# One 64-row-tiled phase per chunk for scores, q/k transposes and x transposes in a gated-attention plus squared-relu kernel

## The chip, the cores and the metric

The kernel runs on one core of one Trainium2 chip. The time is device time of one execution in microseconds (us); lower is better. Every kernel was run four times, three of them interleaved with runs of the kernel before on the same chip. A ratio is the mean time of one kernel's fast runs over the mean of the other's of the same rounds, so it is not quite the ratio of the medians that stand beside it. The rounds ran on different chips, and the median of the kernel before was 196.66 to 198.9 us in them, so runs of different rounds are compared by their ratios or by their profiled spans. Times inside a run are read from its one profiled execution, in which the span from first to last instruction is about 2 us shorter than the device time.

Engines are named as the profile names them: PE (matmul), PEld (weight load), DVE (vector), ACT (activation), POOL, SP. PSUM is the memory that PE writes, in banks of 2 KiB per partition.

## The reference, cut to what matters

```python
# B=4, H=8, S=768, D=48: a gated linear attention, 32 recurrences over 768 tokens
for t in range(S):
    state = alpha[:, :, t, :, None] * state + einsum('bhd,bhe->bhde', k[:, :, t], v[:, :, t])
    y[:, :, t] = einsum('bhd,bhde->bhe', q[:, :, t], state)
x = y.transpose(0, 2, 1, 3).reshape(3072, 384)
h = x @ w_in                  # 384 -> 2048
out = maximum(h, 0)**2 @ w_out  # 2048 -> 384
```

Of the kernel before, what the change touches and what calls it, by code (L numbers as in the profile page):

```python
# [8 lines left out]
FP32 = mybir.dt.float32  # L9
BF16 = mybir.dt.bfloat16  # L10
AF = mybir.ActivationFunctionType
ALU = mybir.AluOpType
PSUM = bass.MemoryType.PSUM
# [6 lines left out]
class Slots:  # L20


    def __init__(self, bufs):
        self.bufs, self.release = bufs, []
# [7 lines left out]


class Op:
    def __init__(self, eng, dur, emit, deps=(), prio=0.0, takes=None, gives=None, lat=0.2, at=0.0):
        self.eng, self.dur, self.emit = eng, dur, emit
        self.deps, self.prio = [d for d in deps if d is not None], prio
        self.takes, self.gives, self.lat, self.at = takes, gives, lat, at
        self.start = self.done = None


class Plan:
# [13 lines left out]
    def ready(self, op):  # L56
        t = op.at
        for d in op.deps:
            if d.done is None:
                return None  # L60
            t = max(t, d.done)
        if op.takes is not None:
            best = None
            for sl in op.takes:
                f = sl.free_at()
                if f is not None and (best is None or f < best):
                    best, op.slot = f, sl
            if best is None:
                return None
            t = max(t, best)  # L70
        return t

    def run(self, gate):
        free = self.free
        while any(self.pending.values()):
            best = None
            for eng, ops in self.pending.items():
                t0 = free.get(eng, 0.0)
                pick = None
                fifo = eng in ("DMA",)  # L80
                for op in (ops[:1] if fifo else ops):
                    if not gate(op):
                        continue
                    r = self.ready(op)
                    if r is None:
                        continue
                    key = (max(r, t0), op.prio)
                    if pick is None or key < pick[0]:
                        pick = (key, op)
                if pick is not None and (best is None or pick[0][0] < best[0]):  # L90
                    best = (pick[0][0], eng, pick[1])
            assert best is not None, "nothing can run"
            t, eng, op = best
            for e in op.durs:
                self.pending[e].remove(op)
            op.eng, op.dur = eng, op.durs[eng]
            op.start = t + getattr(op, "late", 0.0)
            free[eng] = t + op.dur
            if eng == "OUT":
                free["DMA"] = max(free.get("DMA", 0.0), t) + op.dur  # L100
            op.done = t + op.dur + op.lat
            if op.takes is not None:
                self.ready(op)
                op.slot.release.append(op.gives if op.gives is not None else op)
            self.order.append(op)
            self.on_pick(op)
        self.order.sort(key=lambda o: o.start)
# [3 lines left out]
def kernel(  # L111
# [10 lines left out]
    nc = tc.nc  # L122
    B, H, S, D = q.shape
    HD = H * D
    P = 128
    DP = 64
    NP = H // 2
# [3 lines left out]
    KT = d_model // P  # L131
    FT = d_ff // P
    NT = n_tok // P
# [14 lines left out]

    ps_sc = ctx.enter_context(tc.tile_pool(name="ps_sc", bufs=1, space=PSUM))
    ps_st = ctx.enter_context(tc.tile_pool(name="ps_st", bufs=1, space=PSUM))  # L150
    banks = [ctx.enter_context(tc.tile_pool(name=f"bank{i}", bufs=1, space=PSUM)) for i in range(5)]

    nc.scalar.preload_act_table_set("natural_log_exp_and_others")

# [2 lines left out]
    ident_bf = consts.tile([P, P], BF16)  # L157
# [12 lines left out]
    w_in_b = consts.tile([P, KT, d_ff], BF16)  # L170
    w_out_b = consts.tile([P, FT, d_model], BF16)

    NBUF = 4
    L_s = big.tile([P, NBUF, H, DP], BF16)
    nc.gpsimd.memset(L_s[:, :, :, D:], 0.0)
    qA_s = big.tile([P, NBUF, H, DP], BF16)
    nc.gpsimd.memset(qA_s[:, :, :, D:], 0.0)
    kI_s = big.tile([P, NBUF, H, DP], BF16)
    nc.gpsimd.memset(kI_s[:, :, :, D:], 0.0)
    ae_s = big.tile([P, NBUF, NP, 2], FP32)  # L180
    nc.vector.memset(ae_s, 0.0)  # L181
    xT_big = big.tile([P, KT, n_tok], BF16)

    def pin(ins):
        tc.keep_in_program_order(ins)
# [4 lines left out]
    def tr(*a):  # L190
        pin(nc.tensor.transpose(*a))  # L191

    plan = Plan()
    sl_sc = Slots(1)
# [3 lines left out]
    GLA_BANKS = sl_bank[0:2]  # L198
    M1_BANKS = sl_bank[2:5]
    M2_BANKS = sl_bank[4:1:-1]  # L200

    def psum(op, shape, dt):
        i = op.slot.bank
        return banks[i].tile(shape, dt, name=f"bank{i}")
    X_SLACK = 0.3
    LD = 1.02
# [3 lines left out]
    def add(eng, dur, emit, *deps, **kw):  # L210
        return plan.add(Op(eng, dur, emit, deps, **kw))
# [26 lines left out]
    def hold_w(d):  # L238
        def e_hold():
            pin(nc.gpsimd.tensor_copy(hold, d["qt"][:, 0, 0:1]))  # L240
        w_gate[:] = [add("POOL", 0.1, e_hold, d["ld_qt"], prio=-6.0)]

    def hold_x(d, i):
# [4 lines left out]
            pin(nc.gpsimd.tensor_copy(d["at"][:, 0, 0:1], w_out_b[:, j, 0:1]))  # L248
        d["go"] = add("POOL", 0.1, e_hold, w_out_ready[i][0], prio=-6.0)

    C = [dict() for _ in range(NT)]
    state = {}

    def add_loads(s):
        d = C[s]
        b, c = divmod(s, NCH)
        for nm, src in srcs:
            def ld(nm=nm, src=src):
                if nm not in d:
                    d[nm] = loads.tile([P, H, D], FP32, name=nm)  # L260
                pin(nc.sync.dma_start(out=d[nm], in_=src[b, c]))
            prev = C[s - LB]["use_" + nm] if s >= LB else None
            d["ld_" + nm] = add("DMA", LD, ld, prev, d.get("go") if nm == "at" else None, lat=2.0, at=0.6)

    def add_chunk(s):
        d = C[s]
        b, c = divmod(s, NCH)
        i = s % NBUF
        L, qA, kI, ae = L_s[:, i], qA_s[:, i], kI_s[:, i], ae_s[:, i]
        old = C[s - NBUF].get("end") if s >= NBUF else None  # L270
        g = dict(prio=-10.0 + s * 0.01)
        last = c == NCH - 1
# [48 lines left out]
        mq = d["use_qt"] = add("DVE", 0.47, e_qA, a_, d["ld_qt"], old, **g)  # L321
        mk = d["use_kt"] = add("DVE", 0.47, e_kI, ai, d["ld_kt"], old, **g)

        def e_p1():
# [2 lines left out]
                tr(d["pT"][:, p, :], qA[:, 2 * p:2 * p + 2, :], ident_bf)  # L327
            for p in range(NP):
                tr(d["pT"][:, NP + p, :], kI[:, 2 * p:2 * p + 2, :], ident_bf)
        p1 = plan.add(Op("PE", 0.47, e_p1, [mq, mk], takes=GLA_BANKS, **g))  # L330

        def e_cp():
            d["qkT"] = work.tile([P, 2 * NP, P], BF16, name="qkT")
            pin(nc.vector.tensor_copy(d["qkT"], d["pT"]))  # L334
        cp = add("DVE", 0.61, e_cp, p1, **g)
        p1.gives = cp

        def e_p2():
            sc = d["sc"] = ps_sc.tile([P, 2, NP, P], FP32, name="sc")
            t = d["qkT"]  # L340
            for p in range(NP):
                for hh in range(2):
                    sl = slice(64 * hh, 64 * hh + 64)
                    mm(sc[:, hh, p, :], lhsT=t[sl, NP + p, :], rhs=t[sl, p, :], start=True, stop=True)
        p2 = plan.add(Op("PE", 0.42, e_p2, [cp], takes=[sl_sc], **g))

        def e_sm(hh):
            if hh == 0:
                d["sm"] = work.tile([P, 2, NP, P], BF16, name="sm")
            pin(nc.vector.tensor_mul(d["sm"][:, hh], d["sc"][:, hh], utri_b.to_broadcast([P, NP, P])))  # L350
        sm0 = add("DVE", 0.6, lambda: e_sm(0), p2, **g)
        sm1 = add("DVE", 0.6, lambda: e_sm(1), p2, sm0, **g)
        p2.gives = sm1

        ps = None
        if not last:
            def e_ps():
# [3 lines left out]
                for p in range(NP):  # L361
                    mm(st[:, p, :], lhsT=kI[:, 2 * p:2 * p + 2, :], rhs=d["vb"][:, 2 * p:2 * p + 2, :],
                       start=(c == 0 and p == 0), stop=True, skip_group_check=True)
            prev = C[s - 1].get("sb") if s else None
            if c == 0 and s:
                prev = C[s - 2]["sb"]
            ps = plan.add(Op("PE", 0.17, e_ps, [mk, vb, ae1, prev], **g))
# [27 lines left out]
        xn = add("ACT", 0.37, e_xn, p3, **g)  # L395
        p3.gives = xn

        def e_p4():
            d["px"] = psum(p4, [P, KT, P], BF16)
            for j in range(KT):  # L400
                tr(d["px"][:, j, :], d["xn"][:, j * P:(j + 1) * P], ident_bf)
        p4 = plan.add(Op("PE", 0.18, e_p4, [xn], takes=GLA_BANKS, **g))

        def e_xT():
            pin(nc.vector.tensor_copy(xT_big[:, :, s * P:(s + 1) * P], d["px"]))  # L405
        d["x"] = add("DVE", 0.27, e_xT, p4, prio=-9.0, lat=0.2 + X_SLACK)
        p4.gives = d["x"]
        d["end"] = d["x"]


    GN = [4, 1, 1, 2, 2, 2, 2, 2, 2, 2, 2, 2]
# [80 lines left out]
    for d in DMA_ORDER + [s for s in range(NT) if s not in DMA_ORDER]:  # L492
        if d == "i":
            load_w_in(len(w_in_ready))
        elif d == "o":
            load_w_out(len(w_out_ready))
        else:
            if d in HOLD_X:
                hold_x(C[d], HOLD_X[d])
            add_loads(d)  # L500
            add_chunk(d)
            if d in HOLD_W:
                hold_w(C[d])
    b1 = b2 = None
    FIRST_PARTS = [[0, 1], [2, 3]]
    for g in range(NG):
# [10 lines left out]
                b2 = add_moe2(g, tt, b2, {}, range(NQ), M2_LAST if g >= NG - 2 else M2_BANKS if g < M1_ALT else [sl_bank[4]])  # L517
        sq[(g, "free")] = b2

    LEAD = 4  # L520

    def gate(op):
        s = getattr(op, "gla", None)
        if s is not None:
            return s <= LEAD + (prog["m1"] + prog["m2"]) / 5.12
        return True
# [54 lines left out]
```

## The kernel before: the parts that the change touches

The tokens are worked in 24 chunks of 128. A chunk of attention goes through these steps, each of which takes PSUM space from one of two banks (`GLA_BANKS`, banks 0 and 1), except for scores and state, which have their own:

- P0: cumulative sums of log alpha (PE), then `A`, `Ainv` and two small `ae` by exp (ACT); then `qA = q*A`, `kI = k*Ainv` (DVE).
- q/k transposes: eight 128x128 transposes (PE) into one bank, then a copy `qkT` (DVE).
- scores: eight matmuls with 64 rows each (PE), then masking `sm` (DVE).
- product: state times q, and `sm` times v (PE), then the copy `xn` (ACT).
- x transposes: three 128x128 transposes of `xn` (PE), then the copy `xT_big` (DVE).

Beside them run the two large matmuls: the first one, `w_in` with `xT_big` (256 columns in most groups), with relu on ACT (`r`) and the square on DVE (`gT`); the second one, `w_out` with `gT` (384 columns). A small planner in the kernel simulates the engines with planned durations and fixes the order of instructions on each engine ahead of time. The hardware then runs each engine's list in that order and waits on semaphores.

```python
banks = [ctx.enter_context(tc.tile_pool(name=f"bank{i}", bufs=1, space=PSUM)) for i in range(5)]
GLA_BANKS = sl_bank[0:2]
def psum(op, shape, dt):
    i = op.slot.bank
    return banks[i].tile(shape, dt, name=f"bank{i}")      # one tile per bank and use
...
def e_p1():                                               # q/k transposes
    d["pT"] = psum(p1, [P, 2 * NP, P], BF16)
    for p in range(NP):
        tr(d["pT"][:, p, :], qA[:, 2 * p:2 * p + 2, :], ident_bf)
    for p in range(NP):
        tr(d["pT"][:, NP + p, :], kI[:, 2 * p:2 * p + 2, :], ident_bf)
...
def e_p2():                                               # scores: pairs of 64 rows
    for p in range(NP):
        for hh in range(2):
            sl = slice(64 * hh, 64 * hh + 64)
            mm(sc[:, hh, p, :], lhsT=t[sl, NP + p, :], rhs=t[sl, p, :], start=True, stop=True)
...
LEAD = 4                                                  # chunks that P0 may run ahead
```

## Time and profile before

| what | value | view |
|---|---|---|
| device time, median | 198.9 us (197.17 to 199.66, 4 runs) | result |
| PE busy | 94% of the span of 195.0 us | page, part 1 |
| chain that ended last | 87% PE | page, part 4 |
| one chunk in the steady part | 7.07 us; PE 7.07, DVE 5.92, ACT 5.68 | windows |
| eight q/k transposes / three x transposes | 0.45 / 0.17 us | chain, start to next |

These are lines of the page of the kernel before: the span, the busy time of each engine, the busy share of PE in 40 slices in tenths, the granted PE clock in tenths, and the chain of work that ended last, by engine (followed back from the last instruction, at each step to what it had waited for).

```profile
span 195.0 us, 5164 instructions
PE 184.1 (94%) x1920; PEld 130.4 (67%) x1924; DVE 138.2 (71%) x360; ACT 130.9 (67%) x379; POOL 24.0 (12%) x49
PE   7888799999999996999999999999999999999993
PEclk9999999999999999999999999999999999999999
PE 87%; DVE 6%; ACT 3%; issue 1%; ACTq 0%
```

The windows view of the kernel before gives the busy time of each engine in a stretch (with the number of instructions), the clock, and the DMA share:

```profile
core 0: us, PE busy (x) PEld busy (x) DVE busy (x) ACT busy (x) POOL busy (x), PEclk, DMA share, GB/s
103.38:110.45 7.07, 7.07 (x83) 5.40 (x81) 5.92 (x16) 5.68 (x16) 0.64 (x1) 1.00 0.97 202
```

From about 78 us on PE never rests, so PE work taken away should be time taken away. DVE has some 1.2 us and ACT 1.4 us to spare per chunk.

Two stretches of the PE timeline of the kernel before follow (start, duration, engine, line, operation, number of instructions, and in brackets the idle time and what ended it). The first is the steady part, from one P0 to the product; the second is chunk 2 to 3 near the start:

```profile
113.95 0.33 PE L188 MATMUL bank<-L_s,utri_b 128*128 128x384 bf16 x1
114.11 0.24 PE L188 MATMUL bank<-ones_col,L_s 128*128 128x1 bf16 x4
114.22 0.49 PE L188 MATMUL bank<-xT_big,w_in_b 128*128 128x256 bf16 x3
114.54 0.33 PE L188 MATMUL bank<-sb,qkT 128*128 128x96 bf16 x4
...
18.77 0.33 PE L188 MATMUL bank<-sb,qkT 128*128 128x96 bf16 x4
18.94 0.56 PE L188 MATMUL bank<-vb,sm 128*128 128x48 bf16 x8
19.70 0.40 PE L191 MATMUL bank<-ident_bf,qA_s 128*128 128x128 bf16 x4 [0.20 <-DVE qA_s L317]
```

In the steady part the product follows P0 after 0.59 us without a wait, although ACT reads P0's bank until 114.88 us. The product is in the other bank. Near the start, the wait of the q transposes ends with their own input (`qA_s`); what they also wait for in the program is an exp that reads their own bank, and it came earlier.

### The profile page before, as it was taken

What the parts mean: (1) busy time and instruction counts of PE and PEld (TensorE: products, weight loads), DVE (VectorE), ACT (ScalarE), POOL (GpSimd) and SP (SyncE); (2) the same over time, 40 slices, a digit from 0 to 9 for tenths busy, and PEclk for the clock granted to TensorE, in tenths of its full rate; (3) what the DMA queues carried; (4) which work ended last, traced back from release to release, by engine and by line L of the source; (5) the groups of instructions that cost most, each with busy time, mean ns of one, the idle gap of its engine ahead of it and who ended that gap; (6) DMA issues with size and microseconds to landing.
All of it is one profiled execution on the core that took longest, in us unless ns stands there. A gap on an engine that the chain in (4) does not pass through costs nothing.

```text
span 195.0 us, 5164 instructions
## 1 busy us (share of the span) xinstructions
PE 184.1 (94%) x1920; PEld 130.4 (67%) x1924; DVE 138.2 (71%) x360; ACT 130.9 (67%) x379; POOL 24.0 (12%) x49
## 2 busy tenths in 40 slices
PE   7888799999999996999999999999999999999993
PEld 2455444666776775777877777777777787777661
DVE  0588646735999699769998888788888788744300
ACT  3366269527797599488877977877887777565510
POOL 5127300401111111120110110110010000000000
PEclk9999999999999999999999999999999999999999
DMA  6998999899999989998999999601101101110022
GB/s 122 218 216 138 174 197 181 131 196 251 219 216 181 196 180 209 184 216 188 214 224 202 201 204 224 134 33 45 40 5 40 40 3 40 44 40 26 20 79 81
DMA packets 107033, 27.07 MB, mean 139 GB/s; under 512 B 100352, under 2 KB 107008, under 8 KB 107008
## 3 DMA queue, kind: packets, MB, share of 16 engines
q1 hardware_dynamic: 103296, 23.60, 56.2%
q0 software_dynamic: 3712, 3.15, 10.9%
q8 instruction: 15, 0.25, 0.5%
q14 instruction: 10, 0.08, 0.2%
HBM read 25.17 MB, written 4.72 MB: 153 GB/s over the span
## 4 chain that ended last, share of the span: by engine, by line
PE 87%; DVE 6%; ACT 3%; issue 1%; ACTq 0%
PE bank L188 75%; PE bank L191 8%; PE sc L188 3%; DVE sm L350 2%; PE st L188 1%; DVE qA_s L317 1%; DVE st L371 1%; DVE kI_s L320 1%; DVE xT_big L405 1%; ACT r L443 1%; DVE qkT L334 1%; ACT A L298 0%; ACT xn L394 0%; ACT sb L376 0%; ACT L_s L275 0%
## 5 line engine op out<-in xcount | busy, mean ns | idle before, releaser
L443 ACT ACTIVATE r<-bank 128x256 bf16<-128x256 f32 (+2 forms) x192 | 69.1, 386 | 21.9 <-PE bank L188 19.1
L188 PE MATMUL bank<-xT_big,w_in_b 128*128 128x256 bf16 (+2 forms) x575 | 79.5, 272 | 0.9 <-ACT r L443 0.4
L188 PE MATMUL bank<-w_out_b,gT 128*128 128x384 bf16 x384 | 74.7, 326 | 0.0
L449 DVE TENSOR_TENSOR gT<-r 128x256 bf16<-128x256 bf16 (+2 forms) x192 | 55.3, 306 | 20.3 <-ACT r L443 19.1
L188 PEld LDWEIGHTS <-w_in_b 128*128 128x128 bf16 x576 | 48.7, 97 | 15.6 <-issue 1.5
L188 PEld LDWEIGHTS <-gT 128*128 128x128 bf16 x384 | 36.2, 98 | 16.9
L350 DVE TENSOR_TENSOR sm<-sc,utri_b 128x512 bf16<-128x512 f32 x48 | 32.4, 685 | 4.5 <-PE sc L188 4.4
L281 POOL CAST vb<-vt 128x384 bf16<-128x384 f32 x24 | 13.9, 577 | 101.9 <-PE bank L188 58.7
L334 DVE COPY qkT<-bank 128x1024 bf16<-128x1024 bf16 x24 | 16.6, 690 | 7.2 <-PE bank L191 7.1
L317 DVE TENSOR_TENSOR qA_s<-qt,A 128x384 bf16<-128x384 f32 x24 | 13.6, 567 | 8.7 <-ACT A L298 8.7
L480 ACT COPY ob<-bank 128x384 f32<-128x384 f32 x22 | 10.5, 478 | 11.0 <-PE bank L188 10.1
L188 PEld LDWEIGHTS <-qkT 64*128 64x128 bf16 (+1 forms) x272 | 10.9, 95 | 9.8 <-DVE gT L449 3.4
L298 ACT ACTIVATE A<-bank 128x384 bf16<-128x384 f32 x24 | 11.8, 493 | 7.7 <-PE bank L188 7.7
L376 ACT CAST sb<-st 128x384 bf16<-128x384 f32 x20 | 9.6, 478 | 10.8 <-DVE st L371 10.7
L394 ACT CAST xn<-bank 128x384 bf16<-128x384 f32 x24 | 11.5, 480 | 5.0 <-PE bank L188 4.9
L275 ACT ACTIVATE L_s<-at 128x384 bf16<-128x384 f32 x24 | 12.5, 524 | 3.6 <-DMA at<-in_alpha_dram 3.5
L320 DVE TENSOR_TENSOR kI_s<-kt,Ainv 128x384 bf16<-128x384 f32 x24 | 13.5, 564 | 0.2
L188 PE MATMUL bank<-warm 128*128 128x512 bf16 x33 | 11.2, 478 | 1.3 <-DVE ae_s L181 1.3
L302 ACT ACTIVATE Ainv<-bank 128x384 bf16<-128x384 f32 x24 | 11.9, 496 | 0.0
L188 PE MATMUL sc<-qkT 64*128 64x128 bf16 x192 | 9.5, 219 | 2.0 <-DVE qkT L334 2.0
L405 DVE COPY xT_big<-bank 128x384 bf16<-128x384 bf16 x24 | 8.4, 351 | 4.0 <-PE bank L191 3.9
L371 DVE TENSOR_TENSOR st<-st,ae_s 128x384 f32<-128x384 f32 x20 | 11.1, 556 | 0.0
(39 smaller groups left out, 128.2 us busy)
## 6 DMA issues: line engine op xcount, KB each, us to landing
at<-in_alpha_dram SPq DMA_DIRECT2D x24, 192.0 KB, 3.8
qt<-in_q_dram SPq DMA_DIRECT2D x24, 192.0 KB, 3.7
kt<-in_k_dram SPq DMA_DIRECT2D x24, 192.0 KB, 3.8
vt<-in_v_dram SPq DMA_DIRECT2D x24, 192.0 KB, 3.9
out_dram<-ob SPq DMA_DIRECT2D x24, 192.0 KB, 2.3
w_in_b<-in_moe_w_in_dram POOLq DMA_DIRECT2D x4, 384.0 KB, 7.3
w_out_b<-in_moe_w_out_dram POOLq DMA_DIRECT2D x4, 384.0 KB, 8.1
```

The source lines that it names most:

```text
L188: pin(nc.tensor.matmul(*a, **kw))
L191: pin(nc.tensor.transpose(*a))
L275: pin(nc.scalar.activation(L[:, :, 0:D], d["at"], AF.Ln))
L281: pin(nc.gpsimd.tensor_copy(d["vb"], d["vt"]))
L302: pin(nc.scalar.activation(d["Ai"], d["pm"][:, 0:HD].rearrange("p (h d) -> p h d", h=H), AF.Exp, scale=-1.0))
L317: pin(nc.vector.tensor_mul(qA[:, :, 0:D], d["qt"], d["A"]))
L320: pin(nc.vector.tensor_mul(kI[:, :, 0:D], d["kt"], d["Ai"]))
L334: pin(nc.vector.tensor_copy(d["qkT"], d["pT"]))
L350: pin(nc.vector.tensor_mul(d["sm"][:, hh], d["sc"][:, hh], utri_b.to_broadcast([P, NP, P])))
L371: pin(nc.vector.tensor_mul(st4, st4, bcast(ae, D)))
L443: pin(nc.scalar.activation(box["r"][:, 0:n], box["ph"][:, 0:n], AF.Relu))
L449: pin(nc.vector.tensor_mul(gT[g][:, f, 0:n], box["r"][:, 0:n], box["r"][:, 0:n]))
```

## The change

The intent: from chunk 11 on, the full-size transposes become pairs of half-token (64-row) transposes that PE runs at once, as it already does for the scores. Because a switch between 128-row and 64-row instructions costs time (PE is 96 ns late at the entry in these traces), they are put into one phase with the scores. Each half writes its own bank, so one phase needs banks 0 and 1 together; the change therefore makes both banks one tile `G`, so that one DVE copy can read both. A tile is a buffer that the kernel declares by name; waits between the instructions that use a tile are put in when the program is built. P0 may run a chunk further ahead (`LEAD` 5, six chunk buffers).

```diff
-    banks = [ctx.enter_context(tc.tile_pool(name=f"bank{i}", bufs=1, space=PSUM)) for i in range(5)]
+    ps_g = ctx.enter_context(tc.tile_pool(name="ps_g", bufs=1, space=PSUM))
+    banks = [None, None] + [ctx.enter_context(tc.tile_pool(name=f"bank{i}", bufs=1, space=PSUM)) for i in range(2, 5)]
-    NBUF = 4
+    NBUF = 6
+    G = ps_g.tile([P, 2, 512], FP32, name="G")
+    G_b = G.bitcast(BF16)
+    G_T = G_b[:, :, 0:8 * 64].rearrange("p h (t c) -> p h t c", c=64)
+    G_x = G_b[:, :, 8 * 64:11 * 64].rearrange("p h (t c) -> p h t c", c=64)
     def psum(op, shape, dt):
         i = op.slot.bank
+        if i < 2:
+            if dt == FP32:
+                return G[:, i, :]
+            return G_b[:, i, 0:shape[1] * P].rearrange("p (t c) -> p t c", c=P)
+    M0 = 11
... (the separate transposes and scores are kept for earlier chunks) ...
+        def e_ph():
+            if nx:
+                for t in range(2 * NP):
+                    src = (nx["qA"] if t < NP else nx["kI"])[:, 2 * (t % NP):2 * (t % NP) + 2, :]
+                    for h in range(2):
+                        sl = slice(64 * h, 64 * h + 64)
+                        tr(G_T[:, h, t, :], src[sl], ident_bf[sl, sl])
+            for t in range(KT):
+                for h in range(2):
+                    sl = slice(64 * h, 64 * h + 64)
+                    tr(G_x[:, h, t, :], pv["xn"][sl, t * P:(t + 1) * P], ident_bf[sl, sl])
+            d["e_sc"]()
... (the planner learns of operations that take both banks; x copy priority -9 to -11) ...
-    LEAD = 4
+    LEAD = 5
```

`G` is used in all 24 chunks, not only from chunk 11 on.

More of the change, by code (lines that the diff above doesn't have):

```diff
@@ L34, with __init__ @@
 class Op:
-    def __init__(self, eng, dur, emit, deps=(), prio=0.0, takes=None, gives=None, lat=0.2, at=0.0):
+    def __init__(self, eng, dur, emit, deps=(), prio=0.0, takes=None, gives=None, lat=0.2, at=0.0, all_of=None):
         self.eng, self.dur, self.emit = eng, dur, emit
@@ L38, in __init__ @@
         self.takes, self.gives, self.lat, self.at = takes, gives, lat, at
+        self.all_of = all_of
         self.start = self.done = None
@@ L61, in ready @@
             t = max(t, d.done)
+        if op.all_of is not None:
+            for sl, _ in op.all_of:
+                f = sl.free_at()
+                if f is None:
+                    return None
+                t = max(t, f)
         if op.takes is not None:
@@ L104, in run @@
                 op.slot.release.append(op.gives if op.gives is not None else op)
+            for sl, gives in op.all_of or ():
+                sl.release.append(gives)
             self.order.append(op)
@@ L329, in e_p1 @@
                 tr(d["pT"][:, NP + p, :], kI[:, 2 * p:2 * p + 2, :], ident_bf)
-        p1 = plan.add(Op("PE", 0.47, e_p1, [mq, mk], takes=GLA_BANKS, **g))
+        d["mq"], d["mk"], d["qA"], d["kI"] = mq, mk, qA, kI
+        joint_t, joint_s = s > M0, s >= M0
+        if not joint_t:
+            p1 = plan.add(Op("PE", 0.47, e_p1, [mq, mk], takes=GLA_BANKS, **g))
         def e_cp():
             d["qkT"] = work.tile([P, 2 * NP, P], BF16, name="qkT")
-            pin(nc.vector.tensor_copy(d["qkT"], d["pT"]))
-        cp = add("DVE", 0.61, e_cp, p1, **g)
-        p1.gives = cp
+            if joint_t:
+                pin(nc.vector.tensor_copy(d["qkT"].rearrange("p t (h c) -> p h t c", h=2), G_T))
+            else:
+                pin(nc.vector.tensor_copy(d["qkT"], d["pT"]))
+        if joint_t:
+            cp = d["cp"] = add("DVE", 0.63, e_cp, C[s - 1]["ph"], C[s - 2]["x"] if "x" in C[s - 2] else None, **g)
+        else:
+            cp = d["cp"] = add("DVE", 0.61, e_cp, p1, **g)
+            p1.gives = cp
         def e_p2():
@@ L344, in e_p2 @@
                     mm(sc[:, hh, p, :], lhsT=t[sl, NP + p, :], rhs=t[sl, p, :], start=True, stop=True)
-        p2 = plan.add(Op("PE", 0.42, e_p2, [cp], takes=[sl_sc], **g))
+        if not joint_s:
+            p2 = plan.add(Op("PE", 0.42, e_p2, [cp], takes=[sl_sc], **g))
+        else:
+            p2 = d["ph"] = Op("PE", 0.20, None, **g)
+        d["e_sc"] = e_p2
         def e_sm(hh):
@@ L352, in add_chunk @@
         sm1 = add("DVE", 0.6, lambda: e_sm(1), p2, sm0, **g)
+        d["sm1"] = sm1
         p2.gives = sm1
@@ L401, in e_p4, with add_phase @@
                 tr(d["px"][:, j, :], d["xn"][:, j * P:(j + 1) * P], ident_bf)
-        p4 = plan.add(Op("PE", 0.18, e_p4, [xn], takes=GLA_BANKS, **g))
-        def e_xT():
-            pin(nc.vector.tensor_copy(xT_big[:, :, s * P:(s + 1) * P], d["px"]))
-        d["x"] = add("DVE", 0.27, e_xT, p4, prio=-9.0, lat=0.2 + X_SLACK)
+        d["xn_op"] = xn
+        joint_x = M0 - 1 <= s < NT - 1
+        if joint_x:
+            p4 = d["ph_x"] = Op("PE", 0.0, None)
+        else:
+            p4 = plan.add(Op("PE", 0.18, e_p4, [xn], takes=GLA_BANKS, **g))
+        def e_xT():
+            xT = xT_big[:, :, s * P:(s + 1) * P]
+            if joint_x:
+                pin(nc.vector.tensor_copy(xT.rearrange("p t (h c) -> p h t c", h=2), G_x))
+            else:
+                pin(nc.vector.tensor_copy(xT, d["px"]))
+        d["x"] = add("DVE", 0.27, e_xT, p4, prio=-11.0, lat=0.2 + X_SLACK)
         p4.gives = d["x"]
         d["end"] = d["x"]
+    def add_phase(s):
+        d, nx, pv = C[s], C[s + 1] if s + 1 < NT else None, C[s - 1]
+        op = d["ph"]
+        def e_ph():
[10 more added lines that the diff above has]
+            d["e_sc"]()
+        op.emit = e_ph
+        op.deps = [d["cp"], pv["xn_op"]] + ([nx["mq"], nx["mk"]] if nx else [])
+        op.dur = 0.41 + 0.09 + (0.23 if nx else 0.0)
+        last = nx["cp"] if nx else pv["x"]
+        op.all_of = [(GLA_BANKS[0], last), (GLA_BANKS[1], last), (sl_sc, d["sm1"])]
+        plan.add(op)
+        pv["x"].deps = [op]
+        if nx:
+            nx["cp"].deps = [op, pv["x"]]
     GN = [4, 1, 1, 2, 2, 2, 2, 2, 2, 2, 2, 2]
@@ L503 @@
                 hold_w(C[d])
+    for s in range(M0, NT):
+        add_phase(s)
     b1 = b2 = None
```

## The prediction

> **What bounds it now.** The page gives PE 94% of 195.0 us; the chain of waits that ended last is 87% PE. By windows of one chunk (103.38 to 110.45 us, 110.45 to 117.52), PE is busy 7.07 of 7.07 us, DVE 5.92, ACT 5.65, clock 1.00, so from about 78 to 172 us PE is the limit and 7.07 us the period. Before that PE has gaps: in the timeline some 2.1 us between 74.9 and 77.7 us (P0, then state, x and q/k transposes, each waiting for ACT), and 2.9 us between 45 and 65 us.
>
> **What the change saves.** In the chain a chunk's eight q/k transposes take 0.45 us, its three x transposes 0.17: 56 ns each. The scores, already 64-row pairs, start 3 ns apart within a pair and 56 ns from pair to pair (N=128). As the Trainium skill says, "TensorE: Matmul & The Clock Gate", Part 3 (row tiles run concurrently, starts about 4 ns apart). Smallest pitches seen: 25 ns (one column), 26 ns (48 columns). Estimate for a 64-column pair: 29 ns, up to 40 if weight loads of the two halves don't overlap fully. Eleven pairs then cost 0.32 to 0.44 us instead of 0.62: 0.2 to 0.29 us a chunk, over 12 to 13 chunks about 3.2 us. Drains don't change: the skill's "TensorEngine Tiling", Key Properties, says a mode switch drains; here about 96 ns before and 120 ns after the scores, once a chunk, in both kernels. DVE copies should keep 0.69 and 0.35 us. The larger lead moves one P0 ahead of 15 matmuls near 74 us and should remove about 1.3 of the 2.1 us gap.
>
> **What it adds.** Banks 0 and 1 become one tile G. In the built program waits now cross the banks. (a) Steady: in five chunks P0 is followed by three 256-column matmuls (0.33 us), then the state-times-q matmul, which now waits for the exp A in the other bank. A ended 0.93 us after P0's start in this trace, the matmul came at 0.59: a stall of 0.38 to 0.5 us; one later P0 waits for xn likewise; two chunks lose 0.1. About 2.7 us. (b) First 25 us, a chain over DVE: the first product matmuls wait for Ainv or ae_s of the next chunk, the next q transposes for xn: 0.3, 0.6, 0.6 us, say 1.3. (c) In the second matmul of group 0 (35 to 43 us) ACT reads one bank between two quarters of one accumulation in the other: twice about 0.7 us, and 0.4 at its start. (d) Between 50 and 78 us several of 0.2 to 0.5; part is absorbed. Together (b) to (d) about 3.4 us.
>
> Nearly all of it is critical. Sum: -3.2 -1.3 +2.7 +3.4 = +1.6 us.
>
> **Prediction:** 200.0 us, range 196.3 to 203.4. Faster by over 2%: 0.08; within 2%: 0.75; slower by over 2%: 0.17.
>
> **What would show it.** Pairs: transposes of 128x64 starting 3 ns apart, 29 ns between pairs. Steady: chunks with the cross wait keep 7.0 to 7.2 us, those without drop to about 6.8. PE waits on "ACT A" right after P0 and, near 36 and 43 us, on Ainv and xn inside the second matmul. The first 512-column matmul of group 0 starts near 26.2 us instead of 24.9.
>
> **What would make it wrong.** Cross-bank waits absorbed by gaps that exist anyway (then 196 to 197); no concurrency of half transposes (then 202 to 203); the strided DVE copy losing speed (over 203).

## The result

The changed kernel takes 209.88 us (208.35 to 210.72, 4 runs) against 198.9 us (197.17 to 199.66): ratio 1.0557, 95% interval 1.0455 to 1.0658. That is slower, and outside the predicted range of 196.3 to 203.4 us.

The same lines of the page of the changed kernel:

```profile
span 206.3 us, 5454 instructions
PE 185.0 (90%) x2055; PEld 127.7 (62%) x2059; DVE 137.4 (67%) x363; ACT 128.1 (62%) x376; POOL 22.8 (11%) x49
PE   7767689898988898689999999999999999999993
PEclk9997999999999999889999999999999999999999
PE 63%; DVE 14%; ACT 12%; issue 4%; SPq 3%; DMA 2%; ACTq 0%; DVEq 0%
```

PE falls from 87% to 63% of the chain, and DVE and ACT come in. The busy shares drop in the first half, and there are two dents in the clock. The clock records put them at 17.87 to 21.28 us and 86.14 to 89.55 us: twice 3.41 us at half clock. The kernel before has none inside its span. The Trainium skill ("TensorE: Matmul & The Clock Gate", Part 1) says that the PE clock drops to half after an idle window, and that a window is 3413 ns. The length agrees with this trace. The window before was not idle, though: by the windows view PE was busy for 1.36 us of the 3.41 us before the second stretch:

```profile
86.14:89.55 3.41, 3.17 (x27) 1.95 (x24) 2.53 (x5) 0.90 (x2) 0.51 (x1) 0.50 1.01 195
82.73:86.14 3.41, 1.36 (x29) 1.32 (x28) 1.97 (x8) 2.77 (x10) 0.50 (x1) 1.00 1.06 210
```

The intended saving is there. The PE timeline of the changed kernel in one phase:

```profile
94.41 0.29 PE L201 MATMUL G<-ident_bf,qA_s 64*128 64x64 bf16 x8
94.54 0.28 PE L201 MATMUL G<-ident_bf,kI_s 64*128 64x64 bf16 x8
94.66 0.25 PE L201 MATMUL G<-ident_bf,xn 64*128 64x64 bf16 x6
94.74 0.39 PE L198 MATMUL sc<-qkT 64*128 64x128 bf16 x8
```

From the first transpose to the first score it takes 330 ns for 22 half transposes (11 pairs, one half of each in the lower and one in the upper 64 rows), 30 ns a pair, in each of the twelve full phases. Before, eleven transposes took 616 ns. That is 0.286 us saved per chunk, 3.4 us in twelve chunks.

The cost shows in the waits. First the PE and then the ACT timeline of the changed kernel, near the start (the same place as before), and in the steady part:

```profile
20.18 0.53 PE L198 MATMUL G<-sb,qkT 128*128 128x96 bf16 x4
20.51 0.52 PE L198 MATMUL G<-vb,sm 128*128 128x48 bf16 x8
21.96 0.38 PE L201 MATMUL G<-ident_bf,qA_s 128*128 128x128 bf16 x4 [0.93 <-ACT xn L428]
...
125.49 0.33 PE L198 MATMUL G<-L_s,utri_b 128*128 128x384 bf16 x1
125.65 0.24 PE L198 MATMUL G<-ones_col,L_s 128*128 128x1 bf16 x4
125.80 0.49 PE L198 MATMUL bank<-xT_big,w_in_b 128*128 128x256 bf16 x3
126.51 0.33 PE L198 MATMUL G<-sb,qkT 128*128 128x96 bf16 x4 [0.22 <-ACT A L318]
```

```profile
19.15 0.50 ACT L322 ACTIVATE Ainv<-G 128x384 bf16<-128x384 f32 x1
21.07 0.17 ACT L325 ACTIVATE ae_s<-G 64x4 f32<-64x4 f32 x1 [1.42 <-PE G L198]
21.25 0.17 ACT L328 ACTIVATE ae_s<-G 64x4 f32<-64x4 f32 x1
21.43 0.48 ACT L428 CAST xn<-G 128x384 bf16<-128x384 f32 x1
```

In the steady part the product, in one bank, waits for the exp `A`, which reads the other bank. It comes 1.02 us after P0 instead of 0.59. Near the start it is a chain across the banks: the small exp `ae_s` waits until PE has written the product into the other bank; `xn` is queued behind both `ae_s`; and the q transposes, which go to the bank that `ae_s` read, wait for `xn`, which reads the other one. Before, they began 0.76 us after the product matmul; now 1.45 us, part of it at half clock.

The waits are in the built program, of which these lines are an extract in short form. The first of two PE operations writes fp32 columns 0 to 383 of `G`, that is bank 0; the second starts at column 512, that is bank 1; and yet:

```
Matmult G<-L_s,utri_b   writes offset 0,   384 columns
Matmult G<-sb,qkT       writes offset 512,  96 columns   waits for ACT: A<-G (reads offset 0, 384 columns)
Activation Ainv<-G      reads  offset 0,   384 columns   waits for PE: G<-vb,sm (writes offset 512)
```

### The profile page after: what moved, and what is told of

The parts are those of the page before. It is cut to its first block, busy times and chain, and to the rows that moved or that the text cites. A ratio compares the mean times of both kernels' runs of the same rounds, so it can differ in the third digit from the quotient of the medians.

```text
span 206.3 us, 5454 instructions
## 1 busy us (share of the span) xinstructions
PE 185.0 (90%) x2055; PEld 127.7 (62%) x2059; DVE 137.4 (67%) x363; ACT 128.1 (62%) x376; POOL 22.8 (11%) x49
## 4 chain that ended last, share of the span: by engine, by line
PE 63%; DVE 14%; ACT 12%; issue 4%; SPq 3%; DMA 2%; ACTq 0%; DVEq 0%
PE bank L198 42%; PE G L198 11%; PE G L201 6%; DVE sm L383 4%; ACT r L512 4%; SPq L281 3%; ACT A L318 3%; DVE gT L518 2%; DVE qkT L360 2%; PE sc L198 2%; ACT xn L428 2%; DMA at<-in_alpha_dram 2%; ACT Ainv L322 2%; PE st L198 1%; DVE st L405 1%
## 5 line engine op out<-in xcount | busy, mean ns | idle before, releaser
L518 DVE TENSOR_TENSOR gT<-r 128x256 bf16<-128x256 bf16 (+2 forms) x192 | 51.7, 294 | 25.2 <-ACT r L512 24.0
L198 PE MATMUL bank<-w_out_b,gT 128*128 128x384 bf16 x320 | 63.4, 328 | 0.0
L198 PEld LDWEIGHTS <-w_in_b 128*128 128x128 bf16 x576 | 50.5, 97 | 18.7 <-issue 3.9
L301 POOL CAST vb<-vt 128x384 bf16<-128x384 f32 x24 | 12.6, 525 | 114.3 <-PE G L198 51.8
L337 DVE TENSOR_TENSOR qA_s<-qt,A 128x384 bf16<-128x384 f32 x24 | 13.6, 566 | 9.8 <-ACT A L318 9.4
L198 PEld LDWEIGHTS <-qkT 64*128 64x128 bf16 (+1 forms) x272 | 11.4, 97 | 12.5 <-issue 6.6
L428 ACT CAST xn<-G 128x384 bf16<-128x384 f32 x24 | 11.4, 476 | 7.3 <-PE G L198 6.2
L360 DVE COPY qkT<-G 128x1024 bf16<-128x1024 bf16 x12 | 8.3, 690 | 10.0 <-PE G L201 6.8
L318 ACT ACTIVATE A<-G 128x384 bf16<-128x384 f32 x24 | 11.8, 491 | 4.2 <-PE G L198 2.5
L322 ACT ACTIVATE Ainv<-G 128x384 bf16<-128x384 f32 x24 | 12.0, 498 | 2.6 <-PE G L198 2.6
L198 PE MATMUL G<-w_out_b,gT 128*128 128x384 bf16 x64 | 12.2, 325 | 1.4 <-ACT Ainv L322 0.6
L405 DVE TENSOR_TENSOR st<-st,ae_s 128x384 f32<-128x384 f32 x20 | 11.1, 557 | 0.0
L201 PE MATMUL G<-ident_bf,qA_s 64*128 64x64 bf16 (+1 forms) x144 | 8.3, 203 | 2.8 <-ACT xn L428 2.6
```

The costliest lines, as they stand in the source:

```text
L198: pin(nc.tensor.matmul(*a, **kw))
L201: pin(nc.tensor.transpose(*a))
L301: pin(nc.gpsimd.tensor_copy(d["vb"], d["vt"]))
L318: pin(nc.scalar.activation(d["A"], d["pm"][:, 0:HD].rearrange("p (h d) -> p h d", h=H), AF.Exp))
L322: pin(nc.scalar.activation(d["Ai"], d["pm"][:, 0:HD].rearrange("p (h d) -> p h d", h=H), AF.Exp, scale=-1.0))
L337: pin(nc.vector.tensor_mul(qA[:, :, 0:D], d["qt"], d["A"]))
```

## The experiments

Theory A: making banks 0 and 1 one tile is what costs, because the waits made for it cross the banks. Rivals: B, the phases themselves cost (mode switches, strided copies, or needing both banks at once); C, the longer lead starves on input or on ACT. Later runs ask why the saving is smaller than the pairs promise.

### Shared tile alone

```diff
 (the kernel before)
-    banks = [ ... for i in range(5)]
+    ps_g = ...; banks = [None, None] + [ ... for i in range(2, 5)]
+    G = ps_g.tile([P, 2, 512], FP32, name="G")   # and psum() returns G[:, i] for banks 0 and 1
```

> The kernel before, with banks 0 and 1 as halves of one tile G and nothing else; the order of instructions on every engine is that of before. Theory A (the shared tile makes work in one bank wait for the other bank): 204 to 209 us, first 512-column matmul of group 0 near 27 us as in the changed kernel (24.9 before), PE waits inside the group-0 second matmul on Ainv and xn. Theory B (the loss comes from the 64-row phases or the longer lead): 197 to 200 us.

Measured: 218.67 us (218.56 to 219.37) against 196.66 us, ratio 1.11 (1.1043 to 1.1158). The order of instructions on every engine is that of the kernel before. So the tile alone costs 22 us, twice what the whole change lost: theory A has the right sign, and far too small a number; B and C are not needed for a loss. The chunk period in the steady part grows from 7.03 us (70.30 us for ten chunks, product of chunk 13 to that of chunk 23) to 7.96 us (79.64 us). The PE timeline of this run shows the two waits of each chunk that make it up:

```profile
112.33 0.33 PE L189 MATMUL G<-sb,qkT 128*128 128x96 bf16 x4 [0.23 <-ACT A L306]
114.89 0.33 PE L192 MATMUL G<-ident_bf,xn 128*128 128x128 bf16 x3 [0.40 <-ACT ae_s L316]
```

Counted from start to start, PE is late by 0.39 and 0.56 us there.

### Longer lead alone

```diff
 (the kernel before)
-    NBUF = 4
+    NBUF = 6
-    LEAD = 4
+    LEAD = 5
-        d["x"] = add("DVE", 0.27, e_xT, p4, prio=-9.0, lat=0.2 + X_SLACK)
+        d["x"] = add("DVE", 0.27, e_xT, p4, prio=-11.0, lat=0.2 + X_SLACK)
```

> The kernel before with LEAD 5, NBUF 6 and the x copy's priority -11, separate banks, no phases. Theory A: 195.5 to 199 us, since the 2.1 us PE gap near 75 us shrinks and nothing else changes. Rival C (the earlier chunk work starves on input DMA or on ACT in 75 to 100 us, where the changed kernel lost 4 us): 202 us or more, with the loss between 75 and 100 us.

Measured: 196.28 us (196.07 to 197.09) against 196.66 us, ratio 0.9965 (0.9902 to 1.0029). No difference is shown; rival C falls. The gap near 75 us stays at 1.8 us (0.83 us before the product, 0.98 us before the x transposes).

### The changed kernel with two tiles in place of one

```diff
 (the changed kernel)
-    G = ps_g.tile([P, 2, 512], FP32, name="G")
+    G = [ps_g.tile([P, 512], FP32, name=f"G{h}") for h in range(2)]
-                pin(nc.vector.tensor_copy(d["qkT"].rearrange("p t (h c) -> p h t c", h=2), G_T))
+                for h in range(2):
+                    pin(nc.vector.tensor_copy(d["qkT"][:, :, 64 * h:64 * h + 64], G_T[h]))
 (the same for the x copy)
```

> The changed kernel with G as two tiles, one for each bank; each phase's two copies become two half copies each; PE and ACT order are those of the changed kernel. Theory A: all cross-bank waits go; first 512-column matmul back near 25 us, 193.5 to 197 us in all, steady period about 6.8 us. Theory B (phases or lead cost the time): stays at 205 us or more.

Measured: 194.8 us (194.53 to 196.13) against 196.66 us, ratio 0.9895 (0.9836 to 0.9954), correct. PE and ACT run exactly the order of the changed kernel; only the waits differ, and DVE has twice as many copies in the phases. This settles A against B: the phases with separate tiles lose nothing, and the cross-bank waits account for 13.6 us (206.34 less 192.74 us, profiled). The PE timeline of this run at the same step of the steady part:

```profile
120.09 0.33 PE L198 MATMUL G<-L_s,utri_b 128*128 128x384 bf16 x1
120.25 0.24 PE L198 MATMUL G<-ones_col,L_s 128*128 128x1 bf16 x4
120.49 0.49 PE L198 MATMUL bank<-xT_big,w_in_b 128*128 128x256 bf16 x3
120.81 0.33 PE L198 MATMUL G<-sb,qkT 128*128 128x96 bf16 x4
```

The product follows P0 after 0.72 us and no longer waits for `A`. The two half copies cost little, by the DVE timeline of this run 0.75 us for `qkT` and 0.42 us for `xT_big` in place of 0.69 and 0.35 us:

```profile
118.00 0.42 DVE L448 COPY xT_big<-G 128x192 bf16<-128x192 bf16 x2
118.94 0.75 DVE L359 COPY qkT<-G 128x512 bf16<-128x512 bf16 x2
```

This is also the fastest kernel by ratio, about 1% faster than the kernel before: the interval is clear of 1. The Trainium skill ("PSUM — Partial Sum Buffer", "PSUM bank collisions raise a hardware error") asks for guards by bank and 32-partition quadrant and says that accesses to different banks run clean. This run agrees: without waits across the two banks its result is correct.

### The changed kernel without phases

```diff
 (the changed kernel)
-    M0 = 11
+    M0 = 99
```

> The changed kernel without phases (threshold 99): shared tile and longer lead remain; its instruction order is that of the run with the lead alone. Theory A: 208 to 213 us, about 3 us slower than the changed kernel because the half-token pairs are lost. Theory B (the phases are what costs): 199 to 203 us.

Measured: 220.16 us (219.15 to 221.17), ratio 1.1168 (1.1091 to 1.1245). A again has the sign and not the size: with the shared tile the phases are worth 10 to 12 us, not 3 (10.3 by the medians, 11.1 by the profiled spans, 12.0 by the ratios). The steady period is 7.97 us here and 6.74 us in the changed kernel (67.43 us for ten chunks). A phase is one visit to `G` in place of separate visits for q/k and for x, so the wait of 0.56 us before the x transposes should go with it (read from the code and the period, not tested alone). The phases hid part of the cost of the tile that came with them.

### Split tiles, LEAD 4; phases from chunk 8; other planned durations

Three attempts to get more out of the version with split tiles:

```diff
 (split tiles; one of:)
-    LEAD = 5
+    LEAD = 4
-    M0 = 11
+    M0 = 8
-        cp = d["cp"] = add("DVE", 0.63, ...)      # and A, Ainv, xn, relu, x copy, phase likewise
+        cp = d["cp"] = add("DVE", 0.75, ...)
```

> The run with split tiles, but LEAD back to 4 (six chunk buffers stay). Theory A (the lead is a side matter, worth 0.4 us in the run with the lead alone): 194.5 to 196 us. Rival (the phases need the longer lead, because a phase wants the next chunk's q and k): 197 us or more, with PE gaps before the phases.

> Split tiles, phases from chunk 8 on instead of 11. If every phase saves what the pairs show (11 pairs at 32 ns instead of 56, 0.27 us), three more phases give 0.8 us: 193.5 to 194.5 us. Rival (before about 78 us ACT and the chain through xn are the limit, and a phase delays the x transposes): 195 us or more.

> Split tiles, and the planner told the durations that the traces show (ACT exp 0.43, xn 0.40, relu a little longer, half copies 0.75 and 0.35, phase 0.11 longer); only the order changes. If the four 0.37 us PE gaps of the split run near 129, 136, 144 and 150 us (a 256-column matmul waiting for relu behind xn, A and Ainv) come from a plan that thinks ACT faster than it is, they go: 193 to 194.3 us. Rival (they come from two banks for the first matmul): about 194.8 us or no clear difference.

Measured against 197.87 us: 199.32 us (199.02 to 199.42), ratio 1.0091 (1.0045 to 1.0137); 200.69 us (200.55 to 202.51), ratio 1.0184 (1.0122 to 1.0247); 198.77 us (198.19 to 199.03), ratio 1.0062 (1.0004 to 1.0119). All three missed what the theories asked for and are slower than the kernel before, by 0.6 to 1.8%. With LEAD 4 the rival's number came true, and its reason only in part: the gap of about 2.1 us near 75 us is there, and a stretch at half clock from 77.56 to 80.97 us follows it. The half clock is hardly part of the loss: the other three runs have mean clocks of 0.998 to 1.0 and take as long (199.02 to 199.42 us, the profiled one 199.36). The rest lies later. The planner ordered the run of `w_in` matmuls differently, and they wait for relu to give their bank free. This is a stretch of that run's PE timeline, where eighteen 256-column matmuls stand in a row (PE is 0.31 us late at the break inside the x12 line as well):

```profile
104.47 1.78 PE L198 MATMUL bank<-xT_big,w_in_b 128*128 128x256 bf16 x12
106.45 0.82 PE L198 MATMUL bank<-xT_big,w_in_b 128*128 128x256 bf16 x6 [0.20 <-ACT r L514]
```

The run with phases from chunk 8 met the rival's number, and its PE timeline shows a wait of the rival's kind: a phase near 70 us stops for 1.33 us after its first transpose, since its other half goes to bank 1, which an exp of a later chunk still reads.

```profile
68.85 0.20 PE L201 MATMUL G<-ident_bf,qA_s 64*128 64x64 bf16 x1
70.38 0.27 PE L201 MATMUL G<-ident_bf,qA_s 64*128 64x64 bf16 x7 [1.33 <-ACT ae_s L328]
```

With other planned durations several waits of about 0.33 us between `w_in` matmuls remain, and new ones come. What follows: one constant moves the order of hundreds of instructions, and against the split version (by ratio) the three cost 3.9, 5.7 and 3.3 us, more than the pairs save. One property of these orders shows in the traces. A group of three 256-column `w_in` matmuls fills a bank, and the groups alternate between two banks. The third group in a row needs the bank of the first, whose relu is not done. From 78 us on, the kernel before never has three groups in a row; the split version has four such places, each waits 0.37 us, and none of its first or second groups waits over 0.19 us. Summed over the third and later groups of a row, these waits are 1.5 us in the split version, 2.9 us with LEAD 4, 4.2 us from chunk 8 and 4.0 us with other durations. That is a count over traces, and it explains a part of the loss; the rest was not isolated.

### Split tiles, halves not paired

```diff
 (split tiles, inside the phase)
-                for t in range(2 * NP):
-                    for h in range(2):
+                for h in range(2):
+                    for t in range(2 * NP):
 (the same for the x transposes)
```

> Split tiles, with the transposes of each phase in another order: all of the lower half first, then all of the upper half, so that neighbours use the same 64 rows. If the saving comes from two halves running at once, pitch becomes about 29 ns for each 64-column transpose (22 of them 0.64 us, as before the change) and the run loses about 0.3 us a chunk: 197 to 199 us. Rival (order does not matter, the engine overlaps them anyway): 194.8 us.

Measured: 196.44 us (196.15 to 197.39) against 197.87 us, ratio 0.9956 (0.9905 to 1.0007; the paired version had 0.9895 in other rounds). Neither number came. From its first transpose to the next 128-row matmul a phase takes 0.78 us here in each of the twelve, in place of 0.65 us with pairs; without any overlap it would have been about 0.96 (an estimate: 0.65 plus the 0.31 us by which 640 ns exceed 330). Twelve times 0.13 us is 1.6 us; the profiled span is 1.5 us longer than that of the paired version (194.21 against 192.74 us). The PE timeline of this run in one phase shows why (in program order all eight lower-half q and k transposes come before the upper-half ones):

```profile
111.83 0.29 PE L201 MATMUL G<-ident_bf,qA_s 64*128 64x64 bf16 x4
111.96 0.19 PE L201 MATMUL G<-ident_bf,kI_s 64*128 64x64 bf16 x1
111.97 0.20 PE L201 MATMUL G<-ident_bf,qA_s 64*128 64x64 bf16 x1
111.99 0.19 PE L201 MATMUL G<-ident_bf,kI_s 64*128 64x64 bf16 x1
112.01 0.19 PE L201 MATMUL G<-ident_bf,qA_s 64*128 64x64 bf16 x1
```

The upper half starts (111.97 us) while the lower half still has k transposes to do (111.99 us and on), and the two streams then alternate. So a phase is longer where the halves overlap less, which is what a saving by overlap predicts, and overlap does not need strict alternation: PE ran ahead in the list with the other half. A phase without any overlap was not measured.

### The changed kernel, first four chunks in two other banks

```diff
 (the changed kernel)
+        gla = sl_bank[2:4] if s < 4 else GLA_BANKS
-        ... takes=GLA_BANKS, **g
+        ... takes=gla, **g
```

> The changed kernel, but chunks 0 to 3 use banks 2 and 3 (two separate tiles, idle until the first matmul of group 0) in place of the halves of G; the order of work before 60 us is the same, later the planner changes it in places. If the cross-bank waits explain the first 25 us, the first 512-column matmul comes at 24.5 to 25.2 us (27.2 in the changed kernel, 24.9 before), without a half-clock stretch near 18 us, and the run takes 207 to 208.5 us. Rival (something else in the changed kernel delays the start): 27 us and about 210 us.

Measured: 205.91 us (205.54 to 206.71) against 197.59 us, ratio 1.0406 (1.0347 to 1.0466). The first 512-column matmul starts at 24.48 us (changed kernel 27.22), and the half-clock stretch near 18 us is gone; one from 82.75 us remains. The cross-bank waits therefore cost 2.7 us before the large matmuls begin. The total came out 1.1 us below the lower end of what was expected; the later order differs from that of the changed kernel, so not all of the difference between the totals belongs to the start.

### Split tiles, a third bank for the first matmul; phases from chunk 13

```diff
 (split tiles; one of:)
-        takes=M1_BANKS if g < M1_ALT else sl_bank[2:4]
+        takes=M1_BANKS if g < M1_ALT else sl_bank[1:4]
-    M0 = 11
+    M0 = 13
```

> Split tiles, and the 256-column first matmul may use a third bank (bank 1, shared with the chunk work) in the later groups. If its 0.37 us gaps behind relu come from having two banks, they shrink and the run takes 192.5 to 194.5 us. Rival (bank 1 is then missing for P0, q/k and the phases): 197 us or more.

> Split tiles, phases from chunk 13 on instead of 11. By the pairs alone two fewer phases cost about 0.5 us: 195 to 195.8 us. Rival (the plan's order decides more than the pairs, as the runs with LEAD 4, from chunk 8 and with other durations did): off by 2 us or more in either direction.

Measured against 197.59 us: third bank 197.5 us (196.17 to 198.75), ratio 0.9993 (0.9902 to 1.0084), so no gain. The waits behind relu mostly go: the third and later groups in a row, 38 here, wait 1.2 us in sum, so the two banks are what made them. But others come in other places, as this line of its PE timeline, where the product waits for a relu that now reads the shared bank (group 0 also starts its second matmul 1.0 us later, at 36.33 in place of 35.33 us):

```profile
135.11 0.33 PE L198 MATMUL G<-sb,qkT 128*128 128x96 bf16 x4 [0.28 <-ACT r L514]
```

The median meets the rival's number, and the line shows the rival's reason in part; but the four runs fall in two pairs (196.17 and 196.38 us at mean clocks of 0.998 and 1.0, 198.62 and 198.75 us at 0.989), and only the slower pair lies at that number. Phases from chunk 13: 196.72 us (196.48 to 197.74), ratio 0.9947 (0.9888 to 1.0005). It was expected at 195 to 195.8 us by the pairs alone and came 0.9 us later, with an interval that just includes no change; but the kernel before was also 0.9 us slower in these rounds than in those of the split version, so this does not speak against the expectation.

## Why the prediction was wrong, point by point

Where the time went is read by the start of the same piece of work in the profiled runs (us):

| start of | before | changed | lead alone | split tiles | changed less split |
|---|---|---|---|---|---|
| first 512-column matmul (group 0) | 24.91 | 27.22 | 24.80 | 24.71 | 2.51 |
| second matmul of group 1 | 58.82 | 64.13 | 58.70 | 58.68 | 5.45 |
| product `vb,sm` of chunk 8 | 68.34 | 75.07 | 68.22 | 68.20 | 6.87 |
| product of chunk 10 | 82.52 | 92.49 | 81.90 | 81.93 | 10.56 |
| product of chunk 23 | 170.86 | 179.98 | 165.22 | 166.67 | 13.31 |
| end | 195.00 | 206.34 | 194.68 | 192.74 | 13.60 |

(With the lead alone the chunk work runs further ahead of the large matmuls from chunk 12 on, so its row for chunk 23 is no saving.) Changed and split run the same order on PE and ACT, so the last column is the cost of the crossing waits.

| term of the sum | predicted | the runs |
|---|---|---|
| half-token pairs | -3.2 | -1.9 (split tiles less lead alone, profiled; medians -1.5) |
| longer lead | -1.3 | -0.3 (lead alone less before, profiled; the interval includes none) |
| (a) steady part | +2.7 | +3.0 (13.60 less 10.56) |
| (b) first 25 us | +1.3 | +2.5 |
| (c) inside the second matmul of group 0 | +1.8 | +1.9 (PE late by 0.41, 0.74 and 0.73 us at 37.6, 38.7 and 46.1 us) |
| (d) rest up to chunk 10 | about +0.3 net | +6.2 (10.56 less 2.51 less 1.9) |
| sum | +1.6 | +11.4 |

- What bounds the kernel: right. With the waits gone, PE work taken away shortened the kernel.
- The mechanism of the loss: right. Waits that cross the two halves of `G` were read from the built program ahead of time, and the split version, with the same order on PE and ACT, shows that they cost the time. In the group-0 second matmul they stand where they were predicted, as the PE timeline of the changed kernel shows (the kernel before runs these twelve matmuls without a break):

```profile
38.25 0.81 PE L198 MATMUL G<-w_out_b,gT 128*128 128x384 bf16 x4 [0.25 <-ACT A L318]
39.64 0.81 PE L198 MATMUL G<-w_out_b,gT 128*128 128x384 bf16 x4 [0.58 <-ACT Ainv L322]
```

- The step that failed is "(d) Between 50 and 78 us several of 0.2 to 0.5; part is absorbed" and with it "Together (b) to (d) about 3.4 us". The three measured 10.6 us, and (d) alone 6.2 us in place of 0.3. Each wait was sized alone, from times of the kernel before, and waits were then taken to disappear in gaps that existed anyway. Since the changed and the split kernel run the same PE order, each PE instruction can be set beside its twin. The lag of the changed kernel grows from 4.3 us at 47.0 us to 10.6 us at 92.3 us, and it never falls back by more than 0.2 us: next to nothing is absorbed. Some fourteen steps of about 0.2 to 0.75 us at waits make 5.0 us of this, most of them waits across the banks, the others for work on ACT or DVE (relu, masking, a copy) that came late itself. Three of them, from the PE timeline of the changed kernel, where the lag grows by 0.56, 0.64 and 0.51 us:

```profile
62.30 0.36 PE L198 MATMUL G<-vb,sm 128*128 128x48 bf16 x8 [0.40 <-ACT Ainv L322]
71.66 0.33 PE L201 MATMUL G<-ident_bf,xn 128*128 128x128 bf16 x3 [0.47 <-DVE qkT L360]
83.98 0.33 PE L198 MATMUL G<-sb,qkT 128*128 128x96 bf16 x4 [1.23 <-ACT Ainv L322]
```

  The other 1.2 us come in the stretch at half clock near 88 us, and the prediction had no clock term at all. Over the whole run the clock is the smaller part: the run with the highest mean clock of the four (0.992) still took 209.12 us.
- "say 1.3" for (b) was half of what it is. The wait for `xn` was seen, but not that `xn` stands behind two `ae_s` that wait for PE (the ACT lines above), nor the half clock from 17.87 us on, in which the lag behind the split run grows by about 1 us up to the product at 20.18 us. The run with the first chunks in other banks moves the start back by 2.7 us.
- "The larger lead ... should remove about 1.3 of the 2.1 us gap": the lead alone is worth 0.3 us, not resolved from zero. P0 did move ahead, but the product still waits near 75 us (0.83 us) and the x transposes wait for `xn` (0.98 us).
- The pairs: the pitch of 29 ns was right (30 ns measured), and so was 0.29 us a chunk. Of 3.4 us, 1.9 us stay. The split run shows four PE waits of 0.37 us, at 129.3, 136.1, 143.6 and 150.4 us, where a third `w_in` group in a row waits for the relu of the first. They sum to 1.5 us, which is about the rest; the changed kernel has four like them, and the kernel before and the lead alone have no three groups in a row. ACT's queue is not what holds them: in all four the relu starts 0.58 to 0.59 us after the first matmul of its group, twice right behind `Ainv` and twice after ACT had been idle for 0.16 us. The run with a third bank took most of these waits away, but not the time, since its order brought others.

## What to carry to other kernels

When two buffers are merged so that one instruction can read both, look at the waits of every other user of the two, not only at the instruction that gains: here a pair of half copies cost 0.13 us a chunk, and the merged tile cost 13.6 us. Do not count on such waits to vanish in gaps that exist anyway: here fourteen small ones added up almost whole, and stretches at half clock came on top. A stalled engine also holds all work queued behind it, as `xn` stood behind `ae_s` near the start. And an optimization should be measured against a kernel that has only its preparation: with the shared tile the phases were worth 10 to 12 us, without it 1.5 to 2.

## What the Trainium skill lacked or had wrong

- "TensorE: Matmul & The Clock Gate", Part 3, says that matmuls are strict FIFO and monotone in start and end. The unpaired run shows otherwise for two row tiles: an upper-half transpose starts at 111.97 us, before lower-half ones that stand earlier in the program (111.99 us and on), and the two streams alternate.
- The same page, Part 4, gives about 275 ns for a 128x128 transpose in a kernel, and says that the full clock does not engage for transposes. Here one is 220 ns long, but back to back they start every 56 ns at the full clock of 1.00; as pairs of 64-row halves, every 30 ns a pair. Here transposes stand among matmuls; whether they alone would bring the full clock, no run shows. No page gives a rate for paired transposes.
- "TensorEngine Tiling (Array Packing)", Key Properties, says that a mode switch drains PE, without a number. In these traces PE is late by 96 ns at the entry to the 64-row part. At the exit the next 128-row matmul starts 148 ns after the last score, about 95 ns more than the 53 ns from one pair of scores to the next (the prediction's 120 ns is more than this reading gives).
- "PSUM — Partial Sum Buffer" asks for guards by bank and quadrant; no page says that the waits made for a tile of two banks can cross the banks. Here they did, for 22 us when only the tile was changed and 13.6 us in the changed kernel.
- "TensorE: Matmul & The Clock Gate", Part 1, gives the half clock after an idle window. Its length agrees with these traces, 3.41 us each time, but the window before need not be idle: PE was busy for 1.66 and 1.36 us of 3.41 before the two stretches of the changed kernel, and for 1.98 us before that of the run with LEAD 4, while the split version kept the full clock after a window with 1.87 us (74.09 to 77.50 us). Where the limit lies, these runs do not show.
